# One exponential for a whole batch of scores, four steps in one buffer, and far scores by eight key blocks

## The chip, the core and the metric

The kernel runs on one core of a Trainium2 chip. A core has five engines that each work through a queue of their own in order: TensorE (PE, matmuls; PEld is its weight load), VectorE (DVE), ScalarE (ACT), GpSimd (POOL) and SyncE (SP), which here issues every DMA. PE writes into PSUM, which has eight banks of 512 float32 columns on 128 partitions; all other tiles lie in SBUF. The metric is the time of one execution on the device in microseconds (us), as the median of three runs.

## What is computed

Two branches read the same `x` (2048 tokens by 512), and a gate of one number for each token mixes them. Branch A is attention with 32 heads of 16 values, in which each query sees the 256 keys that end with itself. Branch B is a gated feed-forward layer of width 1376. All operands are bf16.

```python
def _A_ref(x, wqkv, wo):
    H = 32; Dh = D // H; W = 256
    q, k, v = ...                       # x @ wqkv, by head
    scores = jnp.einsum("bhqd,bhkd->bhqk", q, k) * (Dh ** -0.5)
    mask = (idx[:, None] - idx[None, :] >= 0) & (idx[:, None] - idx[None, :] < W)
    p = _softmax(jnp.where(mask[None, None], scores, -1e9), axis=-1)
    o = jnp.einsum("bhqk,bhkd->bhqd", p, v)
    return (o by token) @ wo
def _B_ref(x, w1, w3, w2):
    return (_silu(x @ w1) * (x @ w3)) @ w2
g = _sigmoid((x * gate_w).sum(-1, keepdims=True))
return g * _A_ref(x, A_wqkv, A_wo) + (1 - g) * _B_ref(x, B_w1, B_w3, B_w2)
```

## The kernel before

The attention runs in four passes `c`, one for each group of eight heads (128 of the 512 columns). In a pass the 2048 tokens are 16 steps `t` of 128 keys, each of two key blocks of 64 (`KB`); four strips `s` of 32 partitions hold two heads each. Four steps make a chunk `tq` of 512 tokens.

- `projections(c, tq)` makes keys, queries and values of a chunk: matmuls into a bank `ch` (L383 for keys and queries, L429 for values). For the later passes the keys go through `kt` (DVE, L404) and two masked copies on POOL into `kbd` (L407); values go to `vbd` by two copies on ACT (L437) and two on DVE (L439).
- `main_batch(c, t)` makes the scores of a step's 128 keys against the 256 queries from the first key of each block on: eight matmuls with 32 contraction rows (L464) into `su`, a PSUM tile of four banks, one for each strip. Two exponentials on ACT (L469) take two banks each into the step's tile `E`, and one DVE operation (L476) masks the diagonal. In the last step of a pass the matmuls are 128 columns wide.
- `far_batch(c, g)` makes the scores of the far edge of the window for two steps, four key blocks of 64 queries each: sixteen matmuls (L499) into the same `su`, an exponential for each step (L504), and for each step two selections on POOL (L512) that zero what is out of the window.
- `pv(c, i)` multiplies the probabilities of up to three steps with the values for query tile `i`: up to 24 matmuls of 34 columns (L542) into `ch`, a reciprocal (L550) and a scaling (L553) on DVE into `oc`, and a transposing DMA into `OT` (L559).
- The feed-forward layer, for each of four chunks of tokens, has eleven blocks of width 128 (the last 96): four matmuls into `gps`, four into `ups` (both L603), a tanh on ACT (L608), two products on DVE (L612, L616); then for each 128 tokens eleven matmuls (L638) into `ch` and a scaling on DVE into `bsb` (L642).
- The output projection of 128 tokens is four matmuls (L662) that read `OT` of all four passes, an addition of `bsb` on DVE (L666), and a DMA to the output (L669).

There is a single `su`, a single `gps` and `ups`, two `ch` and six `E`. Nothing of this is looped in program order: `Plan` holds every operation with an engine, a cost, a due time and the buffers that it takes and frees, and `emit` simulates the engines to write one fixed order for each queue. An operation that could start earliest goes first, and among those within 0.02 us of it the one due first (L85, L86). Due times come from `at(c, t)` for attention and from `ffn_due`, which spreads the feed-forward work evenly from `TF0` to `TF1`. The costs and due times thus decide the order, and not the time on the chip.

```python
            rows = [r for r in lists[eng] if r[0] <= first + 0.02]
            est, op = min(rows, key=lambda r: (r[1].due, r[1].seq))
```

A score batch takes `su` and both its exponentials free it, so the matmuls of the next batch stand in PE's queue behind other work, which covers the exponentials.

Of the kernel before, what the change touches and what calls it, by code (L numbers as in the profile page):

```python
# [8 lines left out]
ACT = mybir.ActivationFunctionType  # L9
# [102 lines left out]
def kernel(  # L112
# [26 lines left out]
    NE = 6  # L139
# [32 lines left out]
    E = [pp.tile([P, 4, 2, 384], BF16, name=f"E_{i}") for i in range(NE)]  # L172
# [11 lines left out]
    plan = Plan({"su": 1, "g": 1, "u": 1, "ch": 2, "E": NE, "kt": 2, "tt": 2, "h1": 2,  # L184
# [28 lines left out]
    def constants4():  # L213
        for i in range(NE):
            nc.gpsimd.memset(E[i][:, :, 0, 320:384], 0.0)
        v5 = vbd[:].rearrange("p k s (a d) -> p (k s) a d", a=2)
        nc.vector.memset(vbd[:, 0:NKB // 2], 0.0)
        nc.vector.memset(vbd[:, NKB // 2:NKB], 0.0)
        nc.gpsimd.memset(v5[0:KB, :, 0, DH:DH + 1], 1.0)
        nc.gpsimd.memset(v5[KB:P, :, 1, DH:DH + 1], 1.0)  # L220
# [46 lines left out]
    T0, TA, TF0, TF1 = 12.0, 218.0, 6.0, 252.0  # L267
# [98 lines left out]
    def projections(c, tq):  # L366
# [3 lines left out]
        if c:  # L370
            war = [su_ops[(c - 1, t)] for t in range(4 * tq, 4 * tq + 4)]
            war += [far_ops.get((c - 1, g)) for g in (2 * tq, 2 * tq + 1)]
            vwar = [pv_ops[(c - 1, i)] for i in range(4 * tq, min(NT, 4 * tq + 6))]
            qwar = [su_ops[(c - 1, t)] for t in range(max(0, 4 * tq - 3), 4 * tq + 4)]
            qwar += [far_ops.get((c - 1, g)) for g in range(max(0, 2 * tq - 2), 2 * tq + 2)]
        else:
            vwar, qwar = [], []
# [24 lines left out]
        else:  # L402
# [8 lines left out]
            m0 = add("POOL", 0.65, lambda: kmask(0), [b] + war, due, free=[(kj, "kt")])  # L411
            m1 = add("POOL", 0.65, lambda: kmask(1), [b] + war, due, free=[(kj, "kt")])
            k_ready[(c, tq)] = [m0, m1]

        qj = Job()

        def qev():
            nc.vector.tensor_copy(out=qT[:, tq * 512:(tq + 1) * 512], in_=ch[qj.at["ch"]][:])
        a = add("PE", 0.864, lambda: chain(qj, 0, 4), src + qwar, due, take=[(qj, "ch")])
        q_ready[(c, tq)] = add("DVE", 0.69, qev, [a], due, free=[(qj, "ch")])  # L420
# [30 lines left out]
    def main_batch(c, t):  # L451
        due = at(c, t)
        job = Job()
        ej = ejob[(c, t)] = Job()
# [13 lines left out]
        def ex(h):  # L468
            nc.scalar.activation(  # L469
                out=E[ej.at["E"]][:, 2 * h:2 * h + 2, :, 0:wid],  # L470
                in_=su[:, 2 * h:2 * h + 2, 0:2 * wid].rearrange("p s (a q) -> p s a q", a=2),
                func=ACT.Exp, scale=SCALE)

        def mask():
            e = E[ej.at["E"]][:, :, :, 0:KB].rearrange("p s a q -> p (s a) q")
# [3 lines left out]
        a = add("PE", 0.42 if wid == 256 else 0.31, mm, deps, due, take=[(job, "su")])  # L479
        d = 0.833e-3 * 4 * wid + 0.1  # L480
        x0 = add("ACT", d, lambda: ex(0), [a], due, take=[(ej, "E")], free=[(job, "su")])
        x1 = add("ACT", d, lambda: ex(1), [a, x0], due, free=[(job, "su")])
        su_ops[(c, t)] = a
        return add("DVE", 0.42, mask, [x0, x1], due)

    def far_batch(c, g):
        t1 = 2 * g + 1
        due = at(c, t1) + 0.3
        job = Job()
        tq = min(NTC - 1, (P * (2 * g) + 511) // 512)  # L490
        deps = [q_ready[(c, min(NTC - 1, (KB * (4 * g + j) + 319) // 512))] for j in range(4)]
        deps += k_ready[(c, g // 2)]

        def mm():
            for j in range(4):
                q0 = KB * (4 * g + j) + 256
                for s in range(4):
                    r = slice(32 * s, 32 * s + 32)
                    nc.tensor.matmul(su[:, s, j * KB:(j + 1) * KB],  # L499
                                     lhsT=kbd[r, 4 * g + j, :, :].rearrange("p a k -> p (a k)"),  # L500
                                     rhs=qT[r, q0:q0 + KB], start=True, stop=True)

        def ex(i):
            nc.scalar.activation(  # L504
                out=E[ejob[(c, 2 * g + i)].at["E"]][:, :, :, 256:320],
                in_=su[:, :, i * P:(i + 1) * P].rearrange("p s (a q) -> p s a q", a=2),
                func=ACT.Exp, scale=SCALE)

        def mask(i):
            e = E[ejob[(c, 2 * g + i)].at["E"]][:, :, :, 256:320].rearrange("p s a q -> p (s a) q")  # L510
            for lo in (0, KB):
                nc.gpsimd.affine_select(out=e[lo:lo + KB], in_=e[lo:lo + KB], pattern=[[0, 8], [-1, KB]],  # L512
                                        compare_op=ALU.is_ge, fill=0.0, base=-1, channel_multiplier=1)

        a = add("PE", 0.4, mm, deps + [su_ops[(c, t1)]], due, take=[(job, "su")])
        far_ops[(c, g)] = a
        res = []
        for i in range(2):
            x = add("ACT", 0.54, lambda i=i: ex(i), [a], due, free=[(job, "su")])
            res.append(add("POOL", 1.28, lambda i=i: mask(i), [x], due))  # L520
        return res

    def pv(c, i, main, far):
# [13 lines left out]
        def mm():  # L537
            po = ch[job.at["ch"]]
            for s in range(4):
                for bi, (t, par, off) in enumerate(blocks):  # L540
                    e = E[ejob[(c, t)].at["E"]][:, s].rearrange("p a q -> p (a q)")
# [20 lines left out]
        frees = []  # L562
        if i >= 2:
            frees.append((ejob[(c, i - 2)], "E"))
        if i == NT - 1:
            frees += [(ejob[(c, i - 1)], "E"), (ejob[(c, i)], "E")]
# [6 lines left out]
    for c in range(NDC):  # L573
        main, far = {}, {}
        for tq in range(NTC):
            projections(c, tq)
        for t in range(NT):
            main[t] = main_batch(c, t)
            if t % 2 == 1 and t < NT - 2:
                far[t - 1], far[t] = far_batch(c, t // 2)  # L580
# [12 lines left out]
    for tcb in range(NTC):  # L593
        hj = Job()
        hs = []
        for f in range(NFC):
# [25 lines left out]
            t_ = add("ACT", 0.53, th, [a], due, take=[(job, "tt")])  # L622
# [84 lines left out]
```

## Time and profile before

| what | value |
|---|---|
| median of three runs | 264.02 us (263.87 to 264.11) |
| profiled execution, on the device | 264.46 us |
| its span in the trace | 262.4 us, granted TensorE clock 1.00 |
| PE busy | 249.0 us, 3447 matmuls in the records |
| ACT busy | 190.3 us, 271 instructions |
| DVE busy | 174.8 us, 393 instructions |
| POOL busy | 116.1 us, 157 instructions |

The span runs from the first to the last instruction of one execution; the profiled execution's own time is 2.1 us longer than its span and 0.44 us over the median. A busy time is the time in which an engine worked on at least one instruction. Matmuls overlap in PE, so a matmul's listed duration is longer than the time by which it delays the next one; the distance from one group's start to the next group's start is the better price. "issue" is time in which nothing that the profile shows was waited for. Lines such as L464 are lines of the kernel before.

### The profile page before, as it was taken

What the parts mean: (1) busy time and instruction counts of PE and PEld (TensorE: products, weight loads), DVE (VectorE), ACT (ScalarE), POOL (GpSimd) and SP (SyncE); (2) the same over time, 40 slices, a digit from 0 to 9 for tenths busy, and PEclk for the clock granted to TensorE, in tenths of its full rate; (3) what the DMA queues carried; (4) which work ended last, traced back from release to release, by engine and by line L of the source; (5) the groups of instructions that cost most, each with busy time, mean ns of one, the idle gap of its engine ahead of it and who ended that gap; (6) DMA issues with size and microseconds to landing.
All of it is one profiled execution on the core that took longest, in us unless ns stands there. A gap on an engine that the chain in (4) does not pass through costs nothing.

```text
span 262.4 us, 8242 instructions
## 1 busy us (share of the span) xinstructions
PE 249.0 (95%) x3447; PEld 138.2 (53%) x3501; DVE 174.8 (67%) x393; ACT 190.3 (73%) x271; POOL 116.1 (44%) x157
## 2 busy tenths in 40 slices
PE   8999999999999999999999999999989999999992
PEld 8455564654555555555455445564546454455540
DVE  4576977845578867755487775766468867765652
ACT  3278798787677797777768888777677787776640
POOL 6003223662736635782273683751736233332220
PEclk9999999999999999999999999999999999999999
DMA  7999950000001000000000000000000111110112
GB/s 192 267 246 258 223 132 9 13 12 10 8 8 21 8 8 14 11 8 13 6 18 13 8 10 13 14 12 6 13 8 18 45 34 52 50 33 27 50 52 65
DMA packets 27933, 13.14 MB, mean 50 GB/s; under 512 B 17305, under 2 KB 27897, under 8 KB 27897
## 3 DMA queue, kind: packets, MB, share of 16 engines
q1 hardware_dynamic: 27896, 12.63, 21.6%
q8 instruction: 27, 0.44, 0.7%
q14 instruction: 10, 0.07, 0.1%
HBM read 6.85 MB, written 2.10 MB: 34 GB/s over the span
## 4 chain that ended last, share of the span: by engine, by line
PE 86%; ACT 3%; DVE 3%; DMA 2%; POOL 2%; issue 2%; SPq 0%
PE ch L638 14%; PE ch L542 14%; PE gps L603 14%; PE ups L603 13%; PE ch L383 10%; PE su L464 7%; PE ch L429 5%; PE ch L662 5%; DMA OT<-oc 2%; PE su L499 2%; ACT E L469 2%; POOL kbd L407 1%; PE su L225 1%; POOL E L512 1%; ACT vbd L437 1%
## 5 line engine op out<-in xcount | busy, mean ns | idle before, releaser
L469 ACT ACTIVATE E<-su 128x1024 bf16<-128x1024 f32 (+1 forms) x128 | 122.5, 995 | 28.0 <-PE su L464 27.6
L512 POOL TENSOR_SCALAR_AFFINE_SELECT E<-E 64x512 bf16<-64x512 bf16 x112 | 73.5, 656 | 107.3 <-ACT E L504 87.9
L542 PEld LDWEIGHTS <-E 128*128 128x128 bf16 x1440 | 43.3, 96 | 12.9 <-issue 4.6
L407 POOL TENSOR_SCALAR kbd<-kt,rowsA 128x512 bf16<-128x512 bf16 x24 | 38.3, 1605 | 26.5 <-DVE kt L404 11.9
L603 PEld LDWEIGHTS <-w_sb 128*128 128x128 bf16 (+1 forms) x352 | 31.3, 99 | 33.6 <-issue 4.8
L542 PE MATMUL ch<-vbd,E 128*128 128x34 bf16 x1440 | 46.4, 177 | 0.6 <-POOL E L512 0.4
L603 PE MATMUL gps<-xT,w_sb 128*128 128x512 bf16 (+1 forms) x163 | 43.5, 379 | 1.3 <-DVE h L612 0.5
L603 PE MATMUL ups<-xT,w_sb 128*128 128x512 bf16 (+1 forms) x156 | 43.0, 380 | 1.1 <-issue 0.2
L638 PE MATMUL ch<-w_sb,hT 128*128 128x512 bf16 (+1 forms) x161 | 42.6, 380 | 1.2 <-issue 0.5
L504 ACT ACTIVATE E<-su 128x512 bf16<-128x512 f32 x56 | 30.4, 595 | 13.4 <-PE su L499 12.1
L612 DVE SCALAR_TENSOR_TENSOR h<-tt,gps 128x512 bf16<-128x512 bf16 (+1 forms) x44 | 29.8, 678 | 14.8 <-ACT tt L608 14.1
L476 DVE TENSOR_TENSOR E<-E,mdiag 128x512 bf16<-128x512 bf16 x64 | 27.9, 437 | 16.1 <-ACT E L469 16.0
L608 ACT ACTIVATE tt<-gps 128x512 bf16<-128x512 f32 (+1 forms) x44 | 26.3, 598 | 13.5 <-PE gps L603 12.6
L616 DVE SCALAR_TENSOR_TENSOR hT<-h,ups 128x512 bf16<-128x512 bf16 (+1 forms) x44 | 29.9, 681 | 5.7 <-PE ups L603 4.4
L383 PE MATMUL ch<-xT,wqkv_sb 128*128 128x512 bf16 x126 | 32.5, 380 | 0.1
L464 PE MATMUL su<-qT,kbd 32*128 32x256 bf16 (+1 forms) x512 | 25.0, 269 | 1.6 <-ACT E L469 1.2
L550 DVE RECIPROCAL rden<-ch 128x8 f32<-128x8 f32 x64 | 13.1, 204 | 18.1 <-PE ch L542 17.8
L638 PEld LDWEIGHTS <-hT 128*128 128x128 bf16 (+1 forms) x176 | 14.9, 97 | 16.6 <-issue 2.9
L553 DVE SCALAR_TENSOR_TENSOR oc<-ch,gq,rden 128x128 bf16<-128x128 f32 x64 | 22.3, 349 | 1.5
L383 PEld LDWEIGHTS <-wqkv_sb 128*128 128x128 bf16 x128 | 11.5, 98 | 13.6 <-issue 1.4
L662 PE MATMUL ch<-wo_sb,OT 128*128 128x512 bf16 x60 | 16.1, 380 | 2.3 <-DMA OT<-oc 1.5
L464 PEld LDWEIGHTS <-kbd 32*128 32x128 bf16 x512 | 7.9, 92 | 19.3 <-issue 18.1
(55 smaller groups left out, 154.8 us busy)
## 6 DMA issues: line engine op xcount, KB each, us to landing
out_dram<-ot SPq DMA_DIRECT2D x16, 128.0 KB, 1.8
wqkv_sb<-in_A_wqkv_dram SPq DMA_DIRECT2D x6, 256.0 KB, 5.2
w_sb<-in_B_w_dram SPq DMA_DIRECT2D x1, 1280.0 KB, 7.1
w_sb<-in_B_w_dram SPq DMA_DIRECT2D x2, 608.0 KB, 5.3
w_sb<-in_B_w_dram SPq DMA_DIRECT2D x2, 512.0 KB, 6.8
OT<-oc SPq DMA_TRANSPOSE x64, 2.3
xs<-in_A_x_dram SPq DMA_DIRECT2D x2, 256.0 KB, 3.0
w_sb<-in_B_w_dram SPq DMA_DIRECT2D x2, 256.0 KB, 4.4
```

Of the source, the lines that this page charges most:

```text
L383: nc.tensor.matmul(pst[:], lhsT=wqkv_sb[:, dc, col + c * P:col + (c + 1) * P], rhs=xT[:, dc, tq * 512:(tq + 1) * 512], start=(dc == 0), st ...
L407: nc.gpsimd.tensor_scalar_mul(out=kv[:, :, h, :], in0=kt[kj.at["kt"]][:].rearrange("p (k t) -> p k t", t=KB), scalar1=rowsA[:, h:h + 1])
L464: nc.tensor.matmul(su[:, s, par * wid:(par + 1) * wid], lhsT=kbd[r, 2 * t + par, :, :].rearrange("p a k -> p (a k)"), rhs=qT[r, q0:q0 + wi ...
L469: nc.scalar.activation(out=E[ej.at["E"]][:, 2 * h:2 * h + 2, :, 0:wid], in_=su[:, 2 * h:2 * h + 2, 0:2 * wid].rearrange("p s (a q) -> p s ...
L504: nc.scalar.activation(out=E[ejob[(c, 2 * g + i)].at["E"]][:, :, :, 256:320], in_=su[:, :, i * P:(i + 1) * P].rearrange("p s (a q) -> p s ...
L512: nc.gpsimd.affine_select(out=e[lo:lo + KB], in_=e[lo:lo + KB], pattern=[[0, 8], [-1, KB]], compare_op=ALU.is_ge, fill=0.0, base=-1, chann ...
L542: nc.tensor.matmul(po[:, 34 * s:34 * s + 34], lhsT=e[:, off:off + P], rhs=vbd[:, 2 * t + par, s, :], start=(bi == 0), stop=(bi == len(bloc ...
L603: nc.tensor.matmul(dst[0:fs, :], lhsT=w[:, dc, f * P:f * P + fs], rhs=xT[:, dc, tcb * 512:(tcb + 1) * 512], start=(dc == 0), stop=(dc == N ...
L612: nc.vector.scalar_tensor_tensor(out=h1[job.at["h1"]][0:fs, :], in0=tt[job.at["tt"]][0:fs, :], scalar=1.0, in1=gps[0:fs, :], op0=ALU.add, ...
L616: nc.vector.scalar_tensor_tensor(out=hT[0:fs, f, :], in0=h1[job.at["h1"]][0:fs, :], scalar=0.5, in1=ups[0:fs, :], op0=ALU.mult, op1=ALU.mult)
L638: nc.tensor.matmul(bps[:], lhsT=hT[0:fs, f, mm * P:(mm + 1) * P], rhs=w2_sb[0:fs, f, :], start=(f == 0), stop=(f == NFC - 1))
L662: nc.tensor.matmul(pso[:], lhsT=OT[:, c, m * P:(m + 1) * P], rhs=wo_sb[:, c, :], start=(c == 0), stop=(c == NDC - 1))
```

## The change

The planner stays as it is; what it is given changes, and so the order that it writes changes on every queue.

- `E` becomes two tiles of four steps each, laid out by step, strip, block. A new operation `quad(c, h)` of an engine `EQ` that exists only in the plan takes one at no cost; it is freed by the last `pv` that reads it.
- `main_batch` has one exponential over all four banks of `su`, 128 partitions by 2048, in place of two by 1024.
- `far_batch(c, h)` makes eight key blocks (four in the last chunk of a pass): 32 matmuls into all 512 columns of each bank, one exponential by 2048, and for every two steps two POOL selections by 1024 in place of four by 512. It now stands at the head of its chunk and asks for the queries of the next one.
- Due times and costs: queries of a later chunk are due four steps earlier, plus 4.0; `TF1` is 240.0 in place of 252.0; the plan's costs of the key masks (0.65 to 1.6), the tanh (0.53 to 0.6) and the new operations are set anew.

Numbers of instructions: exponentials of main batches 128 to 64, of far batches 56 to 16, score batches 92 to 80, POOL selections 112 to 56. The number and shapes of the matmuls are the same.

```diff
-    E = [pp.tile([P, 4, 2, 384], BF16, name=f"E_{i}") for i in range(NE)]
+    E = [pp.tile([P, 4, 4, 2, 384], BF16, name=f"E_{i}") for i in range(2)]
...
-    T0, TA, TF0, TF1 = 12.0, 218.0, 6.0, 252.0
+    T0, TA, TF0, TF1 = 12.0, 218.0, 6.0, 240.0
...
-            m0 = add("POOL", 0.65, lambda: kmask(0), [b] + war, due, free=[(kj, "kt")])
-            m1 = add("POOL", 0.65, lambda: kmask(1), [b] + war, due, free=[(kj, "kt")])
+            m0 = add("POOL", 1.6, lambda: kmask(0), [b] + war, due, free=[(kj, "kt")])
+            m1 = add("POOL", 1.6, lambda: kmask(1), [b] + war, due, free=[(kj, "kt")])
...
+        qdue = due if tq == 0 else at(c, 4 * tq - 4) - lead + 4.0
...
+    def quad(c, h):
+
+        job = ejob[(c, h)] = Job()
+        return add("EQ", 0.0, lambda: None, [], at(c, 4 * h) - 1.0, take=[(job, "E")], lat=0.0)
...
-        def ex(h):
+        def ex():
             nc.scalar.activation(
-                out=E[ej.at["E"]][:, 2 * h:2 * h + 2, :, 0:wid],
-                in_=su[:, 2 * h:2 * h + 2, 0:2 * wid].rearrange("p s (a q) -> p s a q", a=2),
+                out=E[ej.at["E"]][:, t % 4, :, :, 0:wid],
+                in_=su[:, :, 0:2 * wid].rearrange("p s (a q) -> p s a q", a=2),
                 func=ACT.Exp, scale=SCALE)
...
-        x0 = add("ACT", d, lambda: ex(0), [a], due, take=[(ej, "E")], free=[(job, "su")])
-        x1 = add("ACT", d, lambda: ex(1), [a, x0], due, free=[(job, "su")])
+        x0 = add("ACT", 1.83 if wid == 256 else 1.0, ex, [a], due, free=[(job, "su")])
...
-    def far_batch(c, g):
-        t1 = 2 * g + 1
-        due = at(c, t1) + 0.3
+    def far_batch(c, h, room):
+
+        due = at(c, 4 * h) + 0.3
...
+        nb = min(8, NKB - 4 - 8 * h)
...
-            for j in range(4):
-                q0 = KB * (4 * g + j) + 256
+            for j in range(nb):
+                q0 = KB * (8 * h + j) + 256
                 for s in range(4):
                     r = slice(32 * s, 32 * s + 32)
-                    nc.tensor.matmul(su[:, s, j * KB:(j + 1) * KB],
-                                     lhsT=kbd[r, 4 * g + j, :, :].rearrange("p a k -> p (a k)"),
+                    col = 256 * (j % 2) + KB * (j // 2)
+                    nc.tensor.matmul(su[:, s, col:col + KB],
+                                     lhsT=kbd[r, 8 * h + j, :, :].rearrange("p a k -> p (a k)"),
                                      rhs=qT[r, q0:q0 + KB], start=True, stop=True)
...
             for lo in (0, KB):
-                nc.gpsimd.affine_select(out=e[lo:lo + KB], in_=e[lo:lo + KB], pattern=[[0, 8], [-1, KB]],
+                nc.gpsimd.affine_select(out=e[lo:lo + KB], in_=e[lo:lo + KB],
+                                        pattern=[[0, 16], [-1, KB]],
...
-        frees = []
-        if i >= 2:
-            frees.append((ejob[(c, i - 2)], "E"))
...
+        frees = [(ejob[(c, h)], "E") for h in range(max(0, i - 2) // 4, i // 4 + 1)]
...
-            t_ = add("ACT", 0.53, th, [a], due, take=[(job, "tt")])
+            t_ = add("ACT", 0.6, th, [a], due, take=[(job, "tt")])
```

## The prediction, made before the changed kernel ran

> **What bounds the kernel now.** I read the page first: the busy times, the chain that ended last, and the groups that the change touches.
>
> ```profile
> PE 249.0 (95%) x3447; PEld 138.2 (53%) x3501; DVE 174.8 (67%) x393; ACT 190.3 (73%) x271; POOL 116.1 (44%) x157
> ...
> PE 86%; ACT 3%; DVE 3%; DMA 2%; POOL 2%; issue 2%; SPq 0%
> ...
> L512 POOL TENSOR_SCALAR_AFFINE_SELECT E<-E 64x512 bf16<-64x512 bf16 x112 | 73.5, 656 | 107.3 <-ACT E L504 87.9
> ...
> L504 ACT ACTIVATE E<-su 128x512 bf16<-128x512 f32 x56 | 30.4, 595 | 13.4 <-PE su L499 12.1
> ```
>
> PE is the bound, and almost without gaps. ACT, the engine that the change relieves most, is off the path for all but 3%. So the question is not what ACT saves, but what PE's queue saves in work and in waits. To price the work I read PE's timeline, where the distance from one group's start to the next is what the group costs.
>
> ```profile
> 65.24 1.03 PE L383 MATMUL ch<-xT,wqkv_sb 128*128 128x512 bf16 x4
> 66.10 1.03 PE L638 MATMUL ch<-w_sb,hT 128*128 128x512 bf16 x4
> 67.06 0.40 PE L464 MATMUL su<-qT,kbd 32*128 32x256 bf16 x8
> 67.39 0.77 PE L542 MATMUL ch<-vbd,E 128*128 128x34 bf16 x24
> ...
> 69.80 0.29 PE L499 MATMUL su<-qT,kbd 32*128 32x64 bf16 x16
> 70.03 0.77 PE L542 MATMUL ch<-vbd,E 128*128 128x34 bf16 x24
> ...
> 74.68 0.29 PE L464 MATMUL su<-qT,kbd 32*128 32x128 bf16 x8 [0.16 <-ACT E L469]
> 74.90 1.04 PE L383 MATMUL ch<-xT,wqkv_sb 128*128 128x512 bf16 x4
> ```
>
> Four matmuls of 512 columns cost 0.86 (65.24 to 66.10), but 0.96 where a score batch comes next (66.10 to 67.06): entering one costs 0.10 (medians over the trace 0.863 and 0.959). A main batch costs 0.33, a narrow one 0.22, a far batch 0.23. The narrow one streams 128 columns less in each of two rounds of four strips, and saves 0.107; so 256 columns for each strip take 0.107, and every score batch holds about 0.12 that doesn't depend on its size (main 0.330 - 2 x 0.107; far 0.228 - 0.107).
>
> Priced so, PE's queue is: 720 matmuls of 512 columns at 0.2157 (155.3), 256 at L429 at 0.0553 (14.2), 1440 of 34 columns at 0.0253 (36.4), 60 main batches at 0.33 and 4 at 0.22 (20.7), 28 far batches at 0.228 (6.4), 92 entries at 0.096 (8.8), gate and opening 7.5: 249.3. The first matmul starts at 1.0, and the last one ends at 258.56 (start 258.34 and 0.22). So 258.56 - 1.0 - 249.3 = 8.2 is waiting, and 262.4 - 258.56 = 3.9 is the last addition and output DMA. Group by group, the 8.2 lies so: 0.9 in the opening, 0.5 at 147 us (a `pv` waits for POOL), 1.6 at 187 to 196 (narrow covers at a change of pass), 0.5 at 204 (an `OT` transfer), 2.2 after 246, and 2.5 in crumbs. The end, on PE's timeline:
>
> ```profile
> 254.45 0.76 PE L542 MATMUL ch<-vbd,E 128*128 128x34 bf16 x24
> 255.39 0.81 PE L662 MATMUL ch<-wo_sb,OT 128*128 128x512 bf16 x2 [0.18 <-DVE ot L666]
> 256.48 1.04 PE L662 MATMUL ch<-wo_sb,OT 128*128 128x512 bf16 x4 [0.28 <-DMA OT<-oc]
> 258.34 0.39 PE L662 MATMUL ch<-wo_sb,OT 128*128 128x512 bf16 x1 [0.82 <-DMA OT<-oc]
> ```
>
> The last `pv` is nearly PE's last work, so its reciprocal, scaling and transfer lie bare: 255.06 to 258.34.
>
> **PE's work.** The far scores need 16 batches in place of 28; matmuls are as many as before. Twelve entries go: 12 x 0.096 = 1.15. Twelve batches of 32 matmuls cost 2 x 0.107 + 0.12 = 0.335 each and four stay at 0.228: 4.93 in place of 6.38, 1.45 less. The price of 32 matmuls isn't in the trace; the other bound is 16 matmuls twice, 0.456, which leaves only the entries (saving 1.15), and below 0.335 there is nothing but the entry and the columns. I take 0.335, since columns explain main, narrow and far batches alike. Saved: 2.6 (1.15 to 2.6); work 246.7.
>
> A rule speaks against the second term. In 0.228 us, 16 far matmuls start, one each 14 ns. The Trainium skill (TensorE: Matmul & The Clock Gate, section "Wait — 56ns, not 53.3ns?") says that starts never come closer than about 25 ns, however few the columns. By it 32 matmuls would take 0.80 as an estimate, twice sixteen, and the saving would be the entries' 1.15. The row is faster than the rule here, so I keep the row.
>
> **The turn of `su`.** From a main batch's start to the next batch's start, PE must leave time for the exponentials. The groups kept apart by shape, and ACT's timeline:
>
> ```profile
> L469 ACT ACTIVATE E<-su 128x1024 bf16<-128x1024 f32 x120 | 118.1, 1022 | 25.8 <-PE su L464 25.5
> ...
> L469 ACT ACTIVATE E<-su 128x512 bf16<-128x512 f32 x8 | 4.3, 594 | 2.2 <-PE su L464 2.2
> ```
> ```profile
> 67.51 1.94 ACT L469 ACTIVATE E<-su 128x1024 bf16<-128x1024 f32 x2 [1.09 <-PE su L464]
> ...
> 72.14 1.02 ACT L469 ACTIVATE E<-su 128x1024 bf16<-128x1024 f32 x1
> 73.18 0.40 ACT L437 CAST vbd<-ch 64x256 bf16<-64x256 f32 x1
> 73.60 1.02 ACT L469 ACTIVATE E<-su 128x1024 bf16<-128x1024 f32 x1
> ```
>
> Before, ACT starts 0.45 after the batch (67.06 to 67.51), two exponentials take 1.94, and PE follows 0.06 later (73.60 + 1.02 to 74.68): 2.45. An exponential by 2048 isn't in the trace. The rows by 512 (594 ns) and by 1024 (1022 ns) give 0.836 ns an element and 0.166 fixed, so 1.88; two overlapped ones (1.94) bound it above, if nothing is new in four banks, and the far rows read all four banks at the same 594 ns. The turn becomes 2.39 for main and full far batches; a step saves only 0.06. It saves nothing where other work covers it already. I walked the new order at the prices above: of 72 turns behind a 256-wide main or a full far batch, 48 leave under 2.85, 40 of them about 2.76, so 0.37 to spare. Three turns fall short: a four-block far batch at 60 us by 0.10, the narrow last step of pass 1 at 126 by 0.25, the first step of pass 2 by 0.75. Sum 1.1, against 1.6 before at 187 to 196.
>
> What stands behind the longer exponential: ACT's tanh (0.60) and value copies (0.38), which could slip between the two halves (a copy at 73.18) and now wait up to 0.9 longer. `gps` or `ch` is then late for the next matmuls. The planner knows the long exponential and spreads the work for it; Tanh and copies fill 26.3 + 12.2 us, 15% of the span, so some 7 of the 48 tight turns find ACT busy, and each can lose 0.60 - 0.37 = 0.23: between 0 and 1.6. I take 0.6, nearer to 0, since the same rigid order lost little before.
>
> **POOL, DVE, SP.** POOL: 656 ns for 64x512 and 236 ns for the selection of 64x64 give 0.94 ns an element, so 1.14 for 64x1024, 56 times: 64 in place of 73.5. A far result is needed first by `pv` of the chunk's third tile: in the new order 8.4 to 11.5 after the far batch in the later passes (6.3 the first time), while turn, exponential and first selections take 0.45 + 1.88 + 2.3 = 4.6, or 7.8 with two key masks (3.2) ahead. The wait at 147 us goes: -0.5. DVE's mask is unchanged, 0.44 behind the exponential: 0.45 + 1.88 + 0.06 + 0.44 + 0.05 = 2.9 from main batch to `pv`, and the order leaves 3.1 or more nearly everywhere, as before. The moved query projections keep their DVE copy (0.69), and the loads of `x` that they need are asked for at the same place as before: PE's first 21 groups are unchanged, so the opening's 0.9 stays. SP has the same 64 transposes in the same sequence; from a `pv` to the `L662` that needs it the order leaves 4.1 or more (4.4 before, and one wait of 0.5): I leave 0.5, up to 1.5.
>
> **The end.** With `TF1` at 240 the planner puts 22 matmuls of L638 and two L662 groups behind the last `pv`: 4.75 + 1.7 of work where 3.3 was bare. What is late next is the scaling of `bsb`: its bank must be free for the next to last L662, 0.2 + 0.75 + 0.06 behind the last-but-one L638 group, with 0.65 of work beside it: 0.4. Waiting after the last score batch falls from 2.2 to 0.5.
>
> **Sum.** Waiting 0.9 + 1.1 + 0.6 + 0.5 (`OT`) + 0.5 (end) + 2.5 of crumbs = 6.1. Span 1.0 + 246.7 + 6.1 + 3.9 = 257.7, against 262.4. The profiled execution took 264.46, 2.06 over its span: 259.8. It stood 0.44 over the median of the runs, so 259.3.
>
> **The rivals.**
> - *The gain is eaten by turns.* ACT's operations can no longer interleave, the 0.37 to spare is used up by a tanh (0.60) that starts first, and the crumbs grow by 2 to 3; PE's work falls by 1.15 only. 261 to 263.5. For it: ACT is 73% busy and the order is rigid. Against: before, the turns had 0.3 to 0.5 to spare too and the crumbs came to 2.5 in all.
> - *The exponential over four banks is slow* (slower than before). If it takes x over 1.88, each of the 48 tight turns loses x - 0.37. At x = 0.47 the whole gain of 4.7 is gone; at 0.5 (2.38 for one) the time is about 265.5, and each further 0.1 adds 4.8. Against: the far exponential reads four banks and writes runs of 64 at the price of two banks.
> - *The change doesn't do what it says.* With four steps in one tile, an exponential could be made to wait for masks or `pv` of a neighbour step. 263 to 266. Against: in the built order the main exponentials wait for PE, and here and there for an earlier operation of ACT itself; the far ones wait for POOL, at the selections of the tile's last use, long done.
>
> **Chances and range.** Forecast 0.70 (257 to 261), eaten gain 0.16, slow exponential 0.09, false waits 0.05. Bounds: with nothing lost at the turns and no `OT` wait (2.2 less), 257.1, and 0.3 fewer crumbs give 256.8; with the far batches at 0.456 (1.45) and 1.85 more waiting, 262.6. Range 256.8 to 262.6. What a measurement of this kernel can tell from no change is 0.2%, 0.5 us: below 263.5 is faster, for the forecast, most of the eaten gain and a little of the rest, 0.86; within 0.2% 0.03; slower 0.11.
>
> **What would show it.** PE busy near 246 with the same number of matmuls; L474 (the new main exponential) at 1.88 mean; a 32-matmul far batch followed by the next group after 0.33 (or 0.46); the last transpose landing while L638 matmuls run; POOL's selections at 1.1. I am wrong if PE idles behind ACT at main batches in more than a few places, or if the exponential by 2048 is over 2.25.

## The result and the profile after

The changed kernel takes 265.01 us (median of 20 runs, 263.2 to 266.2) beside 264.12 for the kernel before (20 runs on the same chips): ratio 1.0033, 95% interval 1.0016 to 1.0049. It is slower by 0.33%, where 259.3 was forecast. The profiled execution took 264.99, with a span of 263.1.

From the page of the changed kernel: its busy times, its chain, and the groups of the new main exponential (L474, here with the four narrow ones), the long selection (L518) and DVE's diagonal mask (L481):

```profile
PE 250.6 (95%) x3452; PEld 138.2 (53%) x3501; DVE 181.7 (69%) x393; ACT 181.5 (69%) x167; POOL 107.0 (41%) x97
...
PE 82%; DVE 8%; ACT 5%; issue 4%
...
L474 ACT ACTIVATE E<-su 128x2048 bf16<-128x2048 f32 x64 | 116.6, 1823 | 42.5 <-PE su L469 42.2
L518 POOL TENSOR_SCALAR_AFFINE_SELECT E<-E 64x1024 bf16<-64x1024 bf16 x56 | 64.9, 1159 | 105.2 <-ACT E L509 102.8
...
L481 DVE TENSOR_TENSOR E<-E,mdiag 128x512 bf16<-128x512 bf16 x64 | 33.0, 515 | 15.8 <-ACT E L474 15.6
```

The mask's group before, when it was L476:

```profile
L476 DVE TENSOR_TENSOR E<-E,mdiag 128x512 bf16<-128x512 bf16 x64 | 27.9, 437 | 16.1 <-ACT E L469 16.0
```

ACT and POOL are relieved, by 9 us each (POOL as forecast). But DVE, which was to be untouched, is busy 7 us longer, and its share of the chain has gone from 3% to 8%. Five of the 7 us are the mask: the same 64 operations of the same shape took 27.9 us before (437 ns each) and take 33.0 now. The end is as forecast, a run of L643 matmuls behind the last `pv` and 0.19 of waiting:

```profile
250.93 0.76 PE L549 MATMUL ch<-vbd,E 128*128 128x34 bf16 x24
...
252.60 5.00 PE L643 MATMUL ch<-w_sb,hT 128*128 128x512 bf16 x22
257.79 1.89 PE L667 MATMUL ch<-wo_sb,OT 128*128 128x512 bf16 x8 [0.19 <-DVE bsb L647]
```

So the work fell (at the prices of the prediction) and the end shrank, and both gains were lost again in between. What PE waits for is seen best at its weight loads, since the probabilities `E` are loaded as weights. In the view of waits for them, two rows (total, times, longest) stand out:

```profile
PEld L549 <- DVE E L481: 1.9, 5, 0.6
PEld L549 <- DVE vbd L439: 1.8, 2, 1.2
```

Before, its weight loads waited 0.2 for the mask, once, and not for `vbd` at all. The timeline shows what happens in the largest case:

```profile
227.85 3.62 POOL L518 TENSOR_SCALAR_AFFINE_SELECT E<-E 64x1024 bf16<-64x1024 bf16 x3
...
229.05 0.59 ACT L613 ACTIVATE tt<-gps 128x512 bf16<-128x512 f32 x1
229.19 1.29 DVE L481 TENSOR_TENSOR E<-E,mdiag 128x512 bf16<-128x512 bf16 x1 [1.56 <-ACT E L474]
...
230.53 0.67 PE L549 MATMUL ch<-vbd,E 128*128 128x34 bf16 x20 [0.52 <-DVE E L481]
```

Three selections run back to back; the second lasts from 229.06 to 230.20. The mask starts at 229.19, when its exponential is done, and ends at 230.47, 0.27 after that selection, where 0.42 after its own start would have been 229.61. It has waited inside its own duration, so no view of waits names POOL. The same shows over all 64 masks: the 41 masks that start while POOL is idle take 420 ns on average (427 at most), and the 23 that start inside a POOL operation take 685 (1287 at most). Eleven of the 23 start inside a selection and take 886 on average; ten of these end 0.27 after it, and the one that starts in its last 0.02 is not longer than alone. The other twelve start inside a key mask of POOL (128x512, 1.57) and take 501; three of them are longer, and these end 0.60 before the key mask does. Before, 52 masks took 418 on average outside, and 12 took 516 inside (869 at most), three of them inside a selection: POOL's selections took 73.5 us in all then, but each lasted 0.66. No other DVE operation shows it. Value copies take 428 ns outside and 428 inside a POOL operation, scalings 349 and 350; all of these read PSUM, while the mask reads two SBUF operands, `E` and `mdiag`.

The Trainium skill has this as a rule (SBUF — State Buffer, section "Who interferes with whom"): a VectorE instruction with two SBUF inputs contends with a GpSimd instruction that reads SBUF, over a pair of ports that it calls an exclusive lock. The trace agrees for the selections, with 1287 ns beside 420; beside the key masks it shows less than a lock for the whole length, since by the records those three masks end 0.60 before the key mask. This was the rule that spoke against the change, and the prediction had not weighed it.

The second row, 1.2 us behind a value copy, lies at the change from pass 1 to pass 2. Timeline and stretches there:

```profile
132.35 0.77 DVE L481 TENSOR_TENSOR E<-E,mdiag 128x512 bf16<-128x512 bf16 x1
132.49 0.75 PE L549 MATMUL ch<-vbd,E 128*128 128x34 bf16 x24 [0.20 <-DVE qT L418]
...
133.85 0.42 DVE L439 CAST vbd<-ch 64x256 bf16<-64x256 f32 x1
134.31 0.35 DVE L560 SCALAR_TENSOR_TENSOR oc<-ch,gq,rden 128x128 bf16<-128x128 f32 x1
...
134.33 0.77 PE L549 MATMUL ch<-vbd,E 128*128 128x34 bf16 x24 [1.09 <-DVE vbd L439]
```
```profile
130.00:134.00 4.00, 2.86 (x54) 1.00 0.05 8
134.00:138.00 4.00, 3.40 (x69) 0.71 0.11 21
138.00:142.00 4.00, 4.00 (x35) 0.87 0.05 8
```

The columns of the stretches are length, PE busy, granted clock, DMA share and GB/s. The values of the new pass were computed at 129.5 into one of the two `ch` banks. Their four copies run one after the other, ACT, ACT, DVE, DVE, behind a narrow exponential on ACT and behind the query copy and a mask on DVE (0.77 in place of 0.42, as it starts inside a key mask), and free the bank only at 134.27. The second `pv` waits 1.09 for it. Then PE's clock falls to half, from 135.65 for 3.41 us: 1.7 us of work lost, more than the wait before it.

### The profile page after: what moved, and what is told of

Same layout as the page of the kernel before. It is cut to its first block, busy times and chain, and to the rows that moved or that the text cites. A ratio compares the mean times of both kernels' runs of the same rounds, so it can differ in the third digit from the quotient of the medians.

```text
span 263.1 us, 8042 instructions
## 1 busy us (share of the span) xinstructions
PE 250.6 (95%) x3452; PEld 138.2 (53%) x3501; DVE 181.7 (69%) x393; ACT 181.5 (69%) x167; POOL 107.0 (41%) x97
## 4 chain that ended last, share of the span: by engine, by line
PE 82%; DVE 8%; ACT 5%; issue 4%
PE ch L643 14%; PE ch L549 13%; PE ups L608 13%; PE gps L608 12%; PE ch L382 10%; PE su L469 7%; PE ch L667 5%; PE ch L429 4%; ACT E L474 3%; DVE E L481 2%; PE su L503 2%; DVE vbd L439 2%; PE su L224 1%; DVE bsb L647 1%; ACT vbd L437 1%
## 5 line engine op out<-in xcount | busy, mean ns | idle before, releaser
L474 ACT ACTIVATE E<-su 128x2048 bf16<-128x2048 f32 x64 | 116.6, 1823 | 42.5 <-PE su L469 42.2
L518 POOL TENSOR_SCALAR_AFFINE_SELECT E<-E 64x1024 bf16<-64x1024 bf16 x56 | 64.9, 1159 | 105.2 <-ACT E L509 102.8
L549 PE MATMUL ch<-vbd,E 128*128 128x34 bf16 x1440 | 47.2, 178 | 2.9 <-DVE E L481 1.2
L406 POOL TENSOR_SCALAR kbd<-kt,rowsA 128x512 bf16<-128x512 bf16 x24 | 37.4, 1569 | 30.5 <-DVE kt L403 27.3
L643 PE MATMUL ch<-w_sb,hT 128*128 128x512 bf16 (+1 forms) x166 | 43.2, 384 | 1.1 <-issue 0.4
L481 DVE TENSOR_TENSOR E<-E,mdiag 128x512 bf16<-128x512 bf16 x64 | 33.0, 515 | 15.8 <-ACT E L474 15.6
L509 ACT ACTIVATE E<-su 128x2048 bf16<-128x2048 f32 (+1 forms) x16 | 26.6, 1661 | 6.9 <-PE su L503 6.9
L643 PEld LDWEIGHTS <-hT 128*128 128x128 bf16 (+1 forms) x176 | 15.5, 98 | 18.3 <-issue 3.7
L647 DVE TENSOR_SCALAR bsb<-ch,omg 128x512 bf16<-128x512 f32 x16 | 11.7, 749 | 12.4 <-PE ch L643 12.2
```

The lines of the kernel that those rows point to most:

```text
L406: nc.gpsimd.tensor_scalar_mul(out=kv[:, :, h, :], in0=kt[kj.at["kt"]][:].rearrange("p (k t) -> p k t", t=KB), scalar1=rowsA[:, h:h + 1])
L474: nc.scalar.activation(out=E[ej.at["E"]][:, t % 4, :, :, 0:wid], in_=su[:, :, 0:2 * wid].rearrange("p s (a q) -> p s a q", a=2), func=ACT. ...
L481: nc.vector.tensor_tensor(out=e, in0=e, in1=mdiag[:, None, :].to_broadcast([P, 8, KB]), op=ALU.min)
L509: nc.scalar.activation(out=E[ej.at["E"]][:, 0:nt, :, :, 256:320].rearrange("p t s a q -> p t (s a) q"), in_=su[:].rearrange("p s (a c) -> ...
L549: nc.tensor.matmul(po[:, 34 * s:34 * s + 34], lhsT=e[:, off:off + P], rhs=vbd[:, 2 * t + par, s, :], start=(bi == 0), stop=(bi == len(bloc ...
L643: nc.tensor.matmul(bps[:], lhsT=hT[0:fs, f, mm * P:(mm + 1) * P], rhs=w2_sb[0:fs, f, :], start=(f == 0), stop=(f == NFC - 1))
```

## Experiments

**The length of the selections.** Two kernels change only the selections on POOL; PE, ACT and DVE have the same sequence as in the changed kernel. The first makes each selection as two by 512:

```diff
-                nc.gpsimd.affine_select(out=e[lo:lo + KB], in_=e[lo:lo + KB],
-                                        pattern=[[0, 16], [-1, KB]],
...
+                for k in (0, 8):
+                    nc.gpsimd.affine_select(out=e[lo:lo + KB, k:k + 8], in_=e[lo:lo + KB, k:k + 8],
+                                            pattern=[[0, 8], [-1, KB]],
...
```

> The changed kernel with each POOL selection by 1024 made as two by 512, in the same places of the same order. Theory 1 (a DVE mask that starts while POOL works stands until POOL's operation ends, and those operations are now 1.14 us): the longest masks fall from 1.29 to under 0.95 us, their mean from 515 to about 460 ns, the PE waits behind masks (1.7 us in the changed kernel) halve, and the time falls by about 1 us to 264. Theory 2 (one stall at the change of pass at 131 to 134 us, and the half clock that follows it): no change, 265. Theory 3 (the undivided exponential makes the copies behind it late, whatever POOL does): no change, 265.

Measured: 262.42 us (6 runs), ratio to before 0.9942 (0.9923 to 0.9962). POOL works more (115.4 in place of 107.0), and the kernel is 2.6 faster than the changed one, which makes it faster than before too; theory 1 had expected 1. The longest mask is 897.

The second leaves a selection of one column group only, so most far probabilities stay unmasked:

```diff
-                nc.gpsimd.affine_select(out=e[lo:lo + KB], in_=e[lo:lo + KB],
-                                        pattern=[[0, 16], [-1, KB]],
+                nc.gpsimd.affine_select(out=e[lo:lo + KB, 0:1], in_=e[lo:lo + KB, 0:1],
+                                        pattern=[[0, 1], [-1, KB]],
```

> The changed kernel with each POOL selection on 64 elements in place of 1024, so most far probabilities stay unmasked; the order of all queues is the same. Theory 1: masks are 0.42 us but for the two or three that meet a key mask of POOL, DVE is busy for 5 us less, and the time falls by 2 to 3 us to 262 to 263. Theory 2: the stall at the change of pass has no selection in it, so the time stays within 0.5 us of 265. Theory 3: within 0.5 us of 265.

Measured: 261.13 (6 runs), ratio 0.9903 (0.9876 to 0.9930), a little below what theory 1 expected. The mask's row of the page, here and in the kernel with 512:

```profile
L481 DVE TENSOR_TENSOR E<-E,mdiag 128x512 bf16<-128x512 bf16 x64 | 27.9, 435 | 17.0 <-ACT E L474 16.6
```
```profile
L481 DVE TENSOR_TENSOR E<-E,mdiag 128x512 bf16<-128x512 bf16 x64 | 30.3, 474 | 16.2 <-ACT E L474 15.8
```

435, 474, 515 ns for selections of 64, 512 and 1024 elements, and 261.1, 262.4, 265.0 us. In the changed kernel's order, then, the long selections are worth 2.6 to 3.9 us (2.4 to 3.4 by the ratios, since the kernel before ran 0.3 faster in that round). A part of this is the half clock, which came less often with shorter selections (counted below).

**Length or load?** The next kernel keeps every selection at 1.14 and adds work to POOL, but starts each just behind a DVE mask, by a one-column copy on POOL that reads what that mask wrote:

```diff
+                def select(lo=lo, t=4 * h + 2 * i + lo // KB):
+                    nc.gpsimd.tensor_copy(out=seen[:], in_=E[ej.at["E"]][:, t % 4, 0, 0, 0:1])
+                    nc.gpsimd.affine_select(out=e[lo:lo + KB], in_=e[lo:lo + KB],
...
+                pair(c, 4 * h + 2 * i + lo // KB, select)
```

> The changed kernel with every long POOL selection (1.14, 56 of them) held back until a DVE mask has just ended: selection n of a chunk follows the mask of the chunk's step n, by a one-column copy on POOL that reads what that mask wrote. PE, DVE and ACT have the same instructions in the same sequence as in the changed kernel; only POOL's sequence moves. Theory 1 (a DVE mask that starts inside a POOL operation waits for its end, and the length of the selection is the price): the selections keep their 1.14, but the masks inside POOL operations fall from 23 to about 8 (those beside the key masks of 1.57), the mask mean from 515 to under 450 ns, and the time to about 261.5, between the 262.4 of the selections by 512 and the 261.1 of the kernel with hardly any selection. Rival (what costs is POOL's occupation: far results that come late for PE): masks get short all the same, but PE now waits for POOL, since each selection starts later, and the time stays at 264 to 266.

Measured: 262.63 (6 runs), ratio 0.9944 (0.9923 to 0.9966). The mask's row:

```profile
L490 DVE TENSOR_TENSOR E<-E,mdiag 128x512 bf16<-128x512 bf16 x64 | 28.9, 451 | 17.8 <-ACT E L483 17.6
```

5 masks over 500 ns in place of 11, and in the view of weight loads `pv` waits for masks 0.5 in all, in place of 1.9. Still 18 masks start while POOL works, against my 8, since the key masks of 1.57 stay and a selection now and then lasts into the next mask (two of the five); but the time is that of the short selections. POOL's load is not the cause; the coincidence is.

**The wait at the pass change.** Planning the two copies on an engine as one should bring them through sooner:

```diff
-        for r, w, h in ((0, 0, 0), (0, 1, 1), (1, 1, 1), (1, 0, 0)):
-            prev = add("ACT" if r == 0 else "DVE", 0.36 if r == 0 else 0.42,
-                       lambda r=r, w=w, h=h: vev(r, w, h), [prev], vdue, free=[(vj, "ch")])
+        for r in range(2):
+            prev = add("ACT" if r == 0 else "DVE", 0.76 if r == 0 else 0.87,
+                       lambda r=r: (vev(r, r, r), vev(r, 1 - r, 1 - r)), [prev], vdue, free=[(vj, "ch")])
```

> The changed kernel with the two value copies of ACT planned as one operation and the two of DVE as one, so that nothing comes between them; the order changes. Theory 2: the second pv at the change of pass no longer waits 1.1 us for its bank, the stretch at half clock behind it goes (3.4 us at half clock, 1.7 us of work), and the time falls by 2 to 3.5 us to 261.5 to 263. Theory 1: masks still wait for POOL, the time falls by 0.5 at most. Theory 3: the DVE copies come earlier everywhere and the waits of under 0.4 us behind them (88, 100, 103, 114 us) go too, 1 us more.

Measured: 263.69 (12 runs), ratio 0.9991 (0.9967 to 1.0015). The wait stayed (1.07 us at 130.5), and others came with the moved sequence (0.88 behind an exponential at 74.4). So this didn't remove what it was meant to. What changed is the clock: only 3 of 12 runs had a mean granted clock of 0.994 or less, against 17 of 20 of the changed kernel. The runs above 0.994 have a median of 263.12, beside 263.31 in the changed kernel: apart from the clock it gained next to nothing.

How long must PE stand still for the half clock? In the kernel before, the second exponential of six main batches was repeated, so that PE waits at known places:

```diff
+        more = {(0, 10): 1, (1, 2): 2, (1, 8): 3, (2, 2): 4, (2, 8): 2, (3, 2): 3}.get((c, t), 0)
...
+            for _ in range(1 + (more if h else 0)):
...
```

> The kernel before with the second exponential of six main batches repeated 1, 2, 3, 4, 2 and 3 times more (pass 0 step 10, pass 1 steps 2 and 8, pass 2 steps 2 and 8, pass 3 step 2); each repeat holds ACT for about 0.92 us more and PE waits for the score banks, 0.5 us for one repeat, 1.4, 2.3 and 3.2 for two, three and four. If a wait of PE of about 1 us can bring the half clock, stretches at half clock stand behind several of the stalls of two repeats and more, and the time is longer by them (1.7 us each) on top of the stalls. If the half clock in the changed kernel came from something else, the granted clock stays at 1.0 until the end.

Measured, in one run of 279.78: PE stood still for 2.01, 2.57, 3.87, 1.46 and 2.88 us at 89.5, 116.0, 155.4, 181.1 and 220.4 (the shortest repetition cost no visible wait). Half clock came after 3.87 and 2.88, for 3.41 us each, and not after 2.57 or less. Its timeline for PE at the longest harmless wait:

```profile
115.97 0.40 PE L464 MATMUL su<-qT,kbd 32*128 32x256 bf16 x8 [2.57 <-ACT E L472]
116.30 1.04 PE L641 MATMUL ch<-w_sb,hT 128*128 128x512 bf16 x4
```

By these rows a wait of 1.09 should have been harmless. It wasn't. In the changed kernel the 3.41 us ahead of the half clock and the 3.41 at half clock are these stretches (length, PE busy and matmuls, clock):

```profile
132.24:135.65 3.41, 2.11 (x92) 1.00 0.00 0
135.65:139.07 3.42, 3.15 (x11) 0.50 0.13 24
```

PE was busy for 2.11 of the first, but with matmuls of `pv` and score batches only, none of 512 columns.

Two things in the traces bear on this. First, the clock changes on a grid: the two stretches at half clock of the kernel with repeated exponentials begin at 156.37 and 221.22, which is 19 times 3.413 apart, and in the changed kernel the clock is full from 5.95 on, 38 times 3.413 before 135.65. Where the grid lies differs from one profiled execution to the next (full clock from 5.95, 5.14 and 4.18 on in three of them). So the same wait can fall into one stretch of the grid with other work around it. Second, PE's busy time in such a stretch does not decide. These are whole stretches of the grid, from the kernel with small selections, the one with held selections, and the one with repeated exponentials:

```profile
130.47:133.88 3.41, 2.27 (x68) 1.00 0.07 14
```
```profile
131.43:134.84 3.41, 2.29 (x89) 1.00 0.02 4
```
```profile
112.00:115.41 3.41, 1.40 (x6) 1.00 0.05 10
```

Half clock followed the second alone. The first two hold the pass change with its wait of 1.0 to 1.1 and are busy for the same time, but the first has four matmuls of 512 columns in it and the second one; the third is busy least, with 2.01 of the wait of 2.57 inside it, and has nothing but such wide ones. So it seems that narrow matmuls count for less than wide ones, and that the place of the grid decides which of them fall into the stretch. What exactly is counted, no run here shows.

**The exponential, and the planner's end.** One kernel issues the main exponential as two halves at the same place of the changed kernel's sequence:

```diff
+            for k in (0, 2):
...
-                out=E[ej.at["E"]][:, t % 4, :, :, 0:wid],
+                    out=E[ej.at["E"]][:, t % 4, k:k + 2, :, 0:wid],
...
```

> The changed kernel with its main exponential issued as two by 1024 again, back to back at the same place of ACT's sequence; all other instructions and their sequence are the same. By the prediction's sum two halves take 1.94 where one takes 1.88, so each turn of su gets 0.06 longer and 40 turns have 0.37 to spare: 0 to 1 us slower, 265.0 to 266.0. Rival (the undivided exponential is what costs in the changed kernel): nothing else can slip between the halves here either, so it expects the same 265 to 266; it would be told by the masks and PE's waits behind DVE being unchanged while ACT's busy time rises by about 10 us. If the time falls under 264, an exponential over four banks has a price that its own duration does not show.

Measured: 265.06 (10 runs), ratio 1.0032 (1.0011 to 1.0053): the changed kernel's time. ACT's busy time rises by 3.6 only, since two overlap. In this sequence one exponential for four banks costs nothing by itself, and brings nothing by itself.

The next is the kernel before with that part alone, planned at 1.83, so that the planner's sequence moves:

```diff
-        x0 = add("ACT", d, lambda: ex(0), [a], due, take=[(ej, "E")], free=[(job, "su")])
-        x1 = add("ACT", d, lambda: ex(1), [a, x0], due, free=[(job, "su")])
+        x0 = add("ACT", 1.83 if wid == 256 else 1.0, ex, [a], due, take=[(ej, "E")], free=[(job, "su")])
```

> The kernel before with one part of the change alone: one exponential by 2048 for the four banks (planned at 1.83, mask at 0.45); E per step, far batches by four blocks, short selections and the late FFN end as before. The planner's sequence moves. By the prediction's sum this part is worth 0.06 a turn at most: 263 to 264.5. Theory 1 (selections are the price of the whole change): masks stay near 437 ns and nothing gets slower than 264.5. Rival (ACT undivided: tanh and value copies come late): 265 to 267, with new PE waits behind ACT of 2 us or more in all.

Measured: 266.10 (5 runs), ratio 1.0080 (1.0065 to 1.0095), outside what my theory expected. Masks are short (432 ns), and PE's waits behind ACT come to 0.4; the rows of its waits that are longer than before:

```profile
PE ch L660 <- DMA OT<-oc: 2.0, 3, 0.8
PE ch L636 <- DVE oc L551: 0.9, 1, 0.9
```

These are waits of another sequence, 2.0 for the last transfers (1.5 before) and 0.9 for a `ch` bank, with smaller ones elsewhere. The time lies where the rival put it, but its sign, 2 us or more of waits behind ACT, isn't there. So the same part is worth 0 in the changed kernel's sequence and costs 2.2 when it moves the sequence of the kernel before: what a part is worth through the planner can't be read from its duration.

Setting the FFN's end (`TF1`) back to 252 in the changed kernel moves the sequence too:

```diff
-    T0, TA, TF0, TF1 = 12.0, 218.0, 6.0, 240.0
+    T0, TA, TF0, TF1 = 12.0, 218.0, 6.0, 252.0
```

> The changed kernel with the planner's end of the FFN (TF1) set back to 252. The planner's sequence moves. Theory 1: the long selections stay, so masks stay near 500 ns with some 20 of them inside POOL operations, and the 2 us at the end come back: 264.5 to 266.5. Rival (the changed order round the pass change at 131 us, which TF1 moved, is the cause of the loss, through the half clock there): the stretch at 130 to 139 us loses its waits of 2 us and its half clock, and the time falls to 262 to 263 although the end is 2 us longer.

Measured: 265.53 (6 runs), ratio 1.0061 (1.0044 to 1.0078). The pass change has no half clock here (clock 0.998 or more in all runs), yet the time is 0.5 above the changed kernel, where theory 1 put it and not the rival: waits of 0.86 at 25.0, 0.59 at 40.9 and 0.99 at 77.5 took its place, and the masks stayed at 515 ns.

**Two by two.** Selections long or held back, each with the changed kernel's planner constants and with others that make the first keys, queries and values of a pass some 10 us earlier. All four leave out the transposing of the DMAs, with plain copies in its place, so their values are not the reference's; the first is the control.

```diff
-            nc.sync.dma_start_transpose(out=OT[:, c, i * P:(i + 1) * P],
-                                        in_=oc[job.at["oc"]][:].rearrange("p h d -> p (h d)"))
+            nc.sync.dma_start(out=OT[:, c, i * P:(i + 1) * P],
+                              in_=oc[job.at["oc"]][:].rearrange("p h d -> p (h d)"))
...
```

The constants of the last two:

```diff
-    T0, TA, TF0, TF1 = 12.0, 218.0, 6.0, 240.0
+    T0, TA, TF0, TF1 = 12.0, 219, 6.0, 238
-        lead = 16.0 if c else 3.0
+        lead = (28.0 if tq == 0 else 16) if c else 3.0
-        qdue = due if tq == 0 else at(c, 4 * tq - 4) - lead + 4.0
+        qdue = due if tq == 0 else at(c, 4 * tq - 4) - lead
-        vdue = due + 1.5
+        vdue = due + 2.0
```

> The control of this group: the changed kernel with its 76 transposing DMAs (12 loads of x, 64 of the attention output) made plain DMAs of the same bytes. The transposing is left out, in this kernel and the three beside it, so the values are not the reference's; every engine has the same instructions in the same sequence as in the changed kernel. If the transposes matter for the time only by when they land (2.3 us from issue), a plain copy that lands no later changes nothing: 264 to 266, with the masks near 515 ns and the half clock at 135 us. Rival (plain copies with rows of 256 bytes land later or load the queue): waits of the output projection for the copies at the end, 0.5 to 2 us more.

> As the control, with the long selections held back until a DVE mask has just ended. 262.6 was measured with the transposes, 2.4 below the changed kernel. Expected: 2 to 3 us below the control, mask mean near 450 ns, and the wait of PV for the value copies of the new pass (1.0 us at 133 us) with the half clock behind it in most runs.

> As the kernel with held selections and plain copies, with other planner constants: lead of a pass's first projections 28 in place of 16, TF1 238, TA 219, queries 4 earlier, values 0.5 later. The planner's sequence moves; the first keys, queries and values of a pass are made some 10 us earlier. Theory 1: the wait at 133 us goes and with it the half clock behind it (3.41 us at half, 1.7 lost): 2 to 3 us below the held kernel, near 260, granted clock over 0.996 in nearly all runs. Rival (waits move elsewhere: the ch banks that the early projections take hold up the second half of the FFN): within 1 us of the held kernel.

> As the control (long selections, not held), with the same moved planner constants; PE, DVE and ACT have the same sequence as in the held kernel with these constants. Theory 1 (masks behind selections are a price of the long selections in any sequence): mask mean 490 to 530 ns, some 20 masks inside POOL operations, PE waits for masks of 1.5 us or more in all: 1 to 2.5 us above the held kernel with these constants. Rival (the loss of the changed kernel was the pass change with its half clock, and the masks mattered only there): within 0.5 of it.

Measured, with the ratio to before and its interval:

| planner constants | long selections | held selections |
|---|---|---|
| the changed kernel's | 264.37 (12 runs), 1.0011 (0.9992 to 1.0030) | 262.23 (6 runs), 0.9930 (0.9906 to 0.9954) |
| early projections | 260.32 (4 runs), 0.9854 (0.9838 to 0.9870) | 260.64 (4 runs), 0.9866 (0.9850 to 0.9881) |

Without early projections holding is worth 2.1 us, as with the transposes (2.4). With them it is worth nothing, and here the rival's number came, against my theory. The masks are as long as ever there, but `pv` waits less; mask row and weight-load waits of the kernel with long selections and early projections:

```profile
L481 DVE TENSOR_TENSOR E<-E,mdiag 128x512 bf16<-128x512 bf16 x64 | 33.1, 518 | 20.6 <-ACT E L474 20.2
```
```profile
PEld L549 <- DVE E L481: 1.3, 4, 0.5
```

518 ns, 16 masks over 500, and 1.3 us of waiting for them in place of 1.9, no wait of `pv` for `vbd`, no half clock on the way (0.997 or more in all eight runs of the lower row). Holding pays its own price there: `pv` now waits for selections that start later.

```profile
PEld L563 <- POOL E L530: 1.2, 2, 0.8
```

Holding also did less there: 17 masks still start inside a POOL operation, and their mean falls only from 518 to 493, where it falls from 513 to 450 in the upper row. So this pair is a weak test of what long masks cost. What the lower row does show is that a sequence with masks as long as the changed kernel's can be 4 us faster: a long mask costs PE only where the sequence has no room for it. Several constants were moved at once, and their shares aren't separated.

**The half clock, over all kernels.** Runs with a mean granted clock of 0.994 or less: 17 of 20 of the changed kernel, 7 of 10 with halves, 7 of 12 with plain copies, 4 of 6 and 5 of 6 held, 2 of 6 with selections by 512, 3 of 6 with small ones, 3 of 12 with the value copies as one, and none of 19 with early projections, the later FFN end or the exponential alone. The mark is not sharp: half clock in the last microseconds lowers the mean too, and the kernel before has 0.994 in 6 of 49 runs. In the changed kernel the median of those 17 runs is 265.27, and of the other three 263.31: 2.0 us, against the 1.7 that 3.41 us at half clock lose. Those three runs are 0.8 below the kernel before.

With the clock set apart in this way, the selections' length still counts:

| mean clock | changed kernel | by 512 | held | small |
|---|---|---|---|---|
| above 0.994 | 263.31 (3 runs) | 262.07 (4) | 261.73 (2) | 260.13 (3) |
| 0.994 or less | 265.27 (17 runs) | 262.91 (2) | 263.13 (4) | 262.18 (3) |

So long selections are worth 1.2 to 3.2 us without half clock, and 2.1 to 3.1 with it, from few runs each. The Trainium skill (TensorE: Matmul & The Clock Gate, section "What's actually happening") puts the fall to half speed after at least one idle window of some 3.4 us, in windows that run freely. The grid of 3.41 us and its changing place agree; that a whole window must be idle does not, with PE busy for 2.11 of the 3.41 us ahead.

**Which version is fastest.** Of the kernels that do the whole computation, the one with selections by 512 is the fastest, 262.42, ahead of both. Early projections with plain copies reach 260.32; with the transposes they were not run, and the kernel before was not given such constants either.

## Why the prediction was wrong

*PE's work: right.* A far batch of 32 matmuls costs 0.344 from its start to the next group (0.335 forecast, 0.456 the other bound), and PE's queue 246.8 in place of 249.3. The rule that was set beside it would have given 0.80 and is not borne out. PE's busy time is 250.6 and not near the 246 that was named as a sign: up to 1.7 of the difference are matmuls at half clock, and in the kernel with small selections, whose profile has full clock until its end, it is 246.9.

*The exponential and the turn: right, and worth nothing.* 1876 ns for a full one (1.88 forecast). PE hardly waits behind ACT at `su`: 0.18 and 0.14 in two places. The 0.6 for ACT kept undivided and most of the 1.1 for short turns did not come. The rival of a slow exponential falls, and so does the rival of false waits: of the 42.5 us that ACT is idle before the main exponentials, 42.2 end with their own score matmuls. The gain eaten by turns falls by its mechanism.

*POOL: right for POOL, wrong for its neighbour.* Selections take 1.14 at the median, and the wait for POOL at 147 us is gone. But the step that failed stands right there: "DVE's mask is unchanged, 0.44 behind the exponential". The selection's length was counted as POOL's time alone, and what it does to DVE was put at nothing without a reason. The mask took 0.515 on average and up to 1.29, where the sum left 2.9 of 3.1 us, a margin of 0.2. The kernel before had four such masks over 500 ns; read as a distribution and not as a mean of 437, its trace held the effect already (two inside a selection, two inside a key mask).

*The pass change: one line missing.* The sum had 0.75 for the first turn of pass 2. What came last there was not the turn (0.18) or the query copy (0.20), but the `ch` bank behind four value copies in a row: 1.09. And the sum had no line for the clock: 1.7 in the profiled execution, and 2.0 between the runs with and without it.

*The end: right.* Waiting fell to about 0.5, behind `bsb` as named.

*The sum.* The miss is 5.7 us (265.0 beside 259.3). By the table above, 1.7 of it goes when only runs without half clock are taken (263.3), 3.2 more with small selections (260.1), and 0.8 stays open. In the profiled execution PE waits 259.5 - 1.0 - 246.8 = 11.7, against 6.1 forecast. It lies so, from group start to group start: 0.7 in the opening, 3.6 from 130 to 139 us with the half clock, some 5 at other places where `pv` or a projection waits behind DVE (weight loads wait 1.9 for masks; much of the rest lies behind other DVE work, and how much of that was itself late through a mask was not traced), 0.5 at the end, 1.9 in crumbs. Not all of the 5 can be put down to long masks: small selections took away 3.9 in all, and the kernel with early projections has the long masks and not the loss.

The range ended at 262.6 because its worst case only added wait terms of kinds already in the sum. The loss came from a coupling of two engines that the sum kept apart, and from the clock.

## What to carry to other kernels

Before making an operation longer on one engine, look for operations on the other engine that lengthen when the two overlap: split their durations by whether they start inside it. A mean hides it, and the wait views do not name it, since it lies inside a duration. And in an order written by a planner, a part's worth is its worth with the sequence held; the moved sequence can be worth more with either sign, and is best judged at its tightest place.

## What the runs showed of the hardware

- A DVE operation with two SBUF operands (the mask, 128x512, 0.42) that starts inside a POOL selection ends 0.27 after it (10 of 11 in the changed kernel): up to 1.29 beside a selection of 1.14. Beside a key mask of POOL (1.57) 3 of 12 lengthen, and end 0.60 before it. DVE operations with a PSUM operand don't lengthen (428 and 428 ns, 349 and 350). The other way, selections that start inside a mask take 1.24 on average and up to 1.39 in place of 1.14 (10 of them); inside other DVE operations they take 1.14.
- Half clock for 3.41 us followed a stretch of 3.41 us with PE busy for 2.11 in narrow matmuls and a longest wait of 1.09, while waits of 1.46 to 2.57 among wide matmuls brought none. The clock changed on a grid of 3.41 us whose place differs between runs; a stretch of it busy for 2.29 with one wide matmul was followed by half clock, and stretches busy for 2.27 with four and 1.40 with six were not.
- An exponential of 128x2048 over four PSUM banks takes 1.876, and two halves back to back cost PE nothing more.
